# LSH attention and a gated FFN on one core: the second half of P's value products moved behind the first-layer products, and the hash in two TensorE passes with an add on VectorE

## The chip, the cores and the metric

One core of one Trainium2 chip. The metric is the device time of one execution in microseconds. The engines are named as in the profile: PE (TensorE; PEld its weight loads), DVE (VectorE), ACT (ScalarE), POOL (GpSimd), and SP, which issues most DMAs.

## The reference

```python
# B, H, S, D = 4, 8, 768, 64;  proj (64, 6);  w_in (512, 2048), w_out (2048, 512)
q_bits = (q @ proj) > 0;  k_bits = (k @ proj) > 0        # 6 bits each
q_bucket = sum(q_bits * 2**n);  k_bucket = sum(k_bits * 2**n)
mask = q_bucket[..., :, None] == k_bucket[..., None, :]
scores = where(mask, q @ k.T / sqrt(D), -1e9)
attn = exp(scores - max);  attn = attn / (sum(attn) + 1e-9)
x = (attn @ v), heads side by side: (3072, 512)
h = x @ w_in;  out = (h * clip(h + 3, 0, 6) / 6) @ w_out
```

The inputs are fp32. A product of full precision is made of TensorE passes in a rounded format (fp32r): each operand is split into a rounded high part and the remainder, its low part, and the products high x high, high x low and low x high are summed.

## The kernel before

**Units.** There are 32 heads with 6 tiles of 128 queries each, so 192 tiles g. The FFN takes x in 12 chunks of 256 tokens, each with 16 steps of the 2048 inner columns. The order of the instructions of PE, DVE, ACT and POOL is the order in which the program writes them; SP's is set by a scheduler.

**The stage of the change.** From tile GT = 102 on, attention and FFN run side by side in *slots* k, in the function `beside_ffn`; in the profile this is about 400 to 812 us. One slot holds one FFN step and one tile of each stage of attention. In PE's order:

- in every second slot (called odd here), the value products `acc` of a pair of tiles u: 12 matmuls of 256 columns
- the first layer `h` (gemm1): 12 matmuls of 256 columns
- in one slot in six, the hash `z` of the next head; such a slot is called a *hash slot*, it is always an odd one
- the second layer `po` (gemm2) of the step before: 6 matmuls of 512 columns
- the scores `s` of tile k + 3: 4 matmuls of 384 columns

The other engines in a slot: DVE takes the minimum of the scores (L396, into `p`); ACT the exponential (L408); DVE transposes `p` in 32 x 32 blocks (L429); DMAs carry it out to DRAM (`fd`) and back into the tile `spare` or `px` in transposed form. There it is split: ACT casts it to the high part `ph` (L475), and the low part `pl` is the difference. P has two halves c of 384 key columns. The half c = 1 is split first: `ph_1` by ACT, `pl_1` by POOL (L477). Then ACT makes the FFN's relu `g` (L683), and after it `ph_0`; `pl_0` is made by DVE (L479). ACT then casts the gate's result to `gb` (L689), DVE makes its low part (L690). After the value products, in the next (even) slot, ACT copies the sum out: `y` (L547).

**The value products** (`values_whole`, L505) are summed in one bank in the order ph_1, ph_0, pl_1, pl_0, three matmuls each, all ahead of the slot's first layer.

**The hash** (`hash_qk`, L325) gives 12 rows for q and 12 for k: each of the 6 projections with both signs. The tiles are q1 = [q high; k high], k2 = [k low; k high], q2 = [q high; q low]. Per half of 384 columns, three passes with the weights pjl (low part of proj), pjk and pjq (high part) are summed in one bank of PSUM. In `bits` (L344) DVE compares the rows with a threshold and multiplies them (L352), one instruction for each half, into rows 64 to 108 of q1. A DMA of 12 rows carries k's bits to the tile `k1`. The scores read them as extra rows of the product. In DVE's order bits stand between pl_0 and gb's low part; then comes the minimum of the next scores.

**K's raw rows** of the head after are loaded by a DMA that is put into the list `moves` and issued at the end of a slot, before the four DMAs of `move` (`spare<-fd`, `px<-fd`).

Of the kernel before, what the change touches and what calls it, by code (L numbers as in the profile page):

```python
# [18 lines left out]
P = 128  # L19
NB = 6  # L20
# [23 lines left out]
def lsh_attention_moe(  # L44
# [31 lines left out]
    def dma(out: bass.AP, in_: bass.AP):  # L76
        nonlocal last
        last = nc.sync.dma_start(out=out, in_=in_)  # L78
# [38 lines left out]


    pjl = cp.tile([P, ZM], F32R, name="pjl")
    pjh = cp.tile([P, ZM + ZK - D], F32R, name="pjh")  # L120
    nc.vector.memset(pjl[:].bitcast(F32), 0.0)
    nc.vector.memset(pjh[:].bitcast(F32), 0.0)
    pjk, pjq = pjh[:, :ZM], pjh[:, ZK - D :]


    nc.vector.memset(thr[:], 0.0)
    nc.vector.memset(val[:], 0.0)
    for r, one, big in ((D, 0, -BIG), (ZK, 1, 1.0)):
# [3 lines left out]
        nc.vector.memset(val[r : r + 2 * NB], big * (1, -1)[1 - one])  # L132
        nc.vector.memset(val[r : r + NB], big * (1, -1)[one])
    nc.vector.memset(three[:], 3.0)

    raw0 = sp.tile([P, S], F32, name="raw0", tag="raw", bufs=1)[:]
    dma(out=raw0, in_=qkT[0, 0])
# [107 lines left out]

    def get_k_rows(i: int):
        b, h = divmod(i, H)
        moves.append(lambda: dma(out=raws[i][D:], in_=qkT[b, h, D:]))

    def get_v(i: int):  # L250
        b, h = divmod(i, H)
# [3 lines left out]
    def hash_weights():  # L255
        for x in range(2):
            c = ZK + (1 - x) * NB
            nc.vector.tensor_scalar_mul(pjh[:, c : c + NB], pr[:], (1.0, -1.0)[x])
        for r, c in ((slice(0, D), D), (slice(D, P), ZK)):
            pos = pjh[r, ZK + NB : ZM]  # L260
            nc.vector.tensor_sub(pjl[r, c + NB : c + 2 * NB], pr[r], pos.bitcast(F32))
            nc.vector.tensor_sub(pjl[r, c : c + NB], pos.bitcast(F32), pr[r])

    def spans(i: int):

# [11 lines left out]

    copied = None
    subs = []
    moves = []  # L280

    def split_qk(i: int, copy):
        nonlocal copied
# [41 lines left out]
    def hash_qk(i: int):  # L325
        k1, k2, q1, q2 = state[i]
        if paced:
            z = zs[i] = [bank([P, HW], f"z{i}_{j}") for j in range(2)]
        else:
            both = pair(f"z{i}")  # L330
            z = zs[i] = [both[:, j, :HW] for j in range(2)]
        for j in range(2):
            c = slice(j * HW, (j + 1) * HW)
            nc.tensor.matmul(z[j][:ZM], lhsT=pjl[:], rhs=q1[:, c], start=True, stop=False)
            nc.tensor.matmul(z[j][:ZM], lhsT=pjk, rhs=k2[:, c], start=False, stop=False)
            nc.tensor.matmul(z[j][:ZM], lhsT=pjq, rhs=q2[:, c], start=False, stop=True)
        if not paced:
            zs[i] = both

    def bits(i: int):  # L340
        k1, k2, q1, q2 = state[i]
        z = zs.pop(i)

        if isinstance(z, list):  # L344
            whole = [(slice(j * HW, (j + 1) * HW), z[j][D:ZM], False) for j in range(2)]
        elif i == 0:
            whole = [(slice(j * HW, (j + 1) * HW), z[D:ZM, j, :HW], False) for j in range(2)]
        else:
            whole = [(slice(0, S), z[D:ZM, :, :HW], True)]
        for c, of, both in whole:  # L350
            to = q1[D:ZM, c]
            nc.vector.tensor_scalar(  # L352
                out=to.rearrange("p (j c) -> p j c", j=2) if both else to, in0=of,
                scalar1=thr[D:ZM], scalar2=val[D:ZM], op0=ALU.is_gt, op1=ALU.mult,
            )
            if i == 0:
                nc.scalar.copy(k1[D : D + 2 * NB, c], q1[ZK:ZM, c].bitcast(F32))  # L357
            elif c.stop == S:
                dma(out=k1[D : D + 2 * NB].bitcast(F32), in_=q1[ZK:ZM].bitcast(F32))
# [145 lines left out]
    def values_whole(u: int):  # L505
        vv = vvs[2 * u // KT]
        acc = accs[u] = bank([P, 2 * P], f"acc{u}")
        both = [parts.pop((u, c)) for c in range(2)]
        first, end = (0, 1, 0), (1, 0, QT - 1)
        for part in range(2):  # L510
            for c in (1, 0):
                for x in range(QT):
                    nc.tensor.matmul(  # L513
                        acc[:], lhsT=vv[:, c * QT + x], rhs=both[c][part][:, x],
                        start=(part, c, x) == first, stop=(part, c, x) == end,
                    )

    adds, fresh = [], []

# [518 lines left out]
    def lead(j: int):  # L1038

        i, t = divmod(j, KT)  # L1040
        n = i + 1
        alone = j <= GF + LA
        if t == 0 and n < NJ:
            split_qk(n, nc.scalar.copy if ffn_on else nc.gpsimd.tensor_copy)
        if t in (1, 4) and not paced:
            add()
        if t == (4 if paced else 2):
            if i:
                split_v(i)
        if t == (3 if paced else 2):  # L1050

            if n + 1 < NJ and n != H + 1:
                get_qk(n + 1)
                if paced:
                    get_k_rows(n + 1)
        if t == (5 if paced else 3) and n < NJ:
            get_v(n)
        hashed = t == 3 and n < NJ and alone and j != GB - 1
        if hashed:
            hash_qk(n)  # L1060
        scores(j)
        if hashed:
            bits(n)
        if t == (5 if paced else 4) and n + 1 < NJ:
            scale_q(n + 1)
# [7 lines left out]

    def value_whole():
        nonlocal vnext
        values_whole(vnext // 2)
        vnext += 2

    def value_half():
        nonlocal vnext  # L1080
# [18 lines left out]
    with tc.manual_schedule(engines={ET.PE, ET.DVE, ET.Activation, ET.Pool}):  # L1099
# [15 lines left out]
        def beside_ffn(k: int):  # L1115

            nonlocal paced, stage, held
            held = False  # L1120
            if k < GT:
                for c in range(2):
                    transp(k, c)
                exponential(k + 1)
            for _ in range(2):
                u = vnext // 2
                if u < NS // 2 and (2 * u < GT or k % 2 and k >= 2 * u + 3):
                    if vnext % 2 == 0 and k >= GT:
                        value_whole()
                        through.append(u)  # L1130
                        break
                    if value_half():
                        through.append(vnext // 2 - 1)
                if k < GT:
                    break
            behind = (k - 1 + LA) % KT == 4
            if GT <= k < NS - 2 and not behind:
                lowest(k + 2)
            go("A")
            if GT <= k < NS - 2 and behind:  # L1140
                lowest(k + 2)
            if k < GT:
                for c in range(2):
                    split_p(k, c, False)
                split_lows()
                while through:
                    output(through.pop(0))
                flip(k + 1)
            if k + 2 < NS:
                if k < GT:  # L1150
                    lowest(k + 2)
                    assert len(side) <= 2
                    opening.pop()()
                if k == GT:
                    go("B")
                    go("C")
                exponential(k + 2)
            paced = True
            multiply()
            if k + 2 < NS:  # L1160
                flip(k + 2)
            split = GT <= k - LT < NS
            if split:
                split_p(k - LT, 1, False)
            go("B")
            if k == NS + LT:
                homes.clear()
            while through and (through[0] < vnext // 2 - 1 or k % 2 == 0 or k < GT):
                output(through.pop(0))
            hashed = k + LA < NS and (k + LA) % KT == 4 and (k + LA) // KT + 1 < NJ  # L1170
            if hashed:
                hash_qk((k + LA) // KT + 1)
            if split:
                amid.append(lambda: (split_p(k - LT, 0, False), split_lows()))
            go("C")
            while amid:
                amid.pop()()
            split_lows()
            if hashed:
                bits((k + LA) // KT + 1)  # L1180
            if k + LA < NS:
                lead(k + LA)
            if moves:
                moves.pop(0)()
            if GT <= k + 1 < NS:
                move(k + 1)

            place_in_chunk = (k - GT) % NFC
            if subs and (k % 2 and (k < GT or place_in_chunk != NFC - 1) or k > GT and place_in_chunk == 0):
                subs.pop(0)()  # L1190
            go("D")
            if k % KT in (1, 3):
                add()

        for k in range(NS + LT + 2):
# [10 lines left out]
                load_first_x()  # L1206
            if k == HK:
                late["x"] = sp.tile([P, S], F32, name="late", tag="raw", bufs=1)
            for c in range(2):
                transp(k, c)  # L1210
            if k + 1 < end:
# [116 lines left out]
```

## Time and profile before

| what | us |
|---|---|
| median of 3 runs | 975.36 (973.79 to 977.28) |
| the profiled execution | 973.11 |
| its span in the profile | 971.3 |
| PE busy | 948.0, 98% of the span |
| DVE busy | 723.5, 74% |
| ACT busy | 625.0, 64% |
| POOL busy | 473.6, 49% |

The granted clock of TensorE was 0.998 of full speed. In a row of the timeline the first two numbers are the start and the length in us; `x6` counts instructions that follow one another on one line; the bracket gives the engine's idle time before the row and what ended it. In a row of a group of instructions, the numbers behind the first bar are the busy time in us and the mean of one in ns, those behind the second bar the idle time before them. In a row of one line's instructions, the three numbers are the shortest, median and longest in ns, and in the indented rows the idle time in us in front of them, by what ended it, and how often. Matmuls overlap, so the time that one of them takes on PE is the distance of the starts.

### The profile page before, as it was taken

What the parts mean: (1) busy time and instruction counts of PE and PEld (TensorE: products, weight loads), DVE (VectorE), ACT (ScalarE), POOL (GpSimd) and SP (SyncE); (2) the same over time, 40 slices, a digit from 0 to 9 for tenths busy, and PEclk for the clock granted to TensorE, in tenths of its full rate; (3) what the DMA queues carried; (4) which work ended last, traced back from release to release, by engine and by line L of the source; (5) the groups of instructions that cost most, each with busy time, mean ns of one, the idle gap of its engine ahead of it and who ended that gap; (6) DMA issues with size and microseconds to landing.
All of it is one profiled execution on the core that took longest, in us unless ns stands there. A gap on an engine that the chain in (4) does not pass through costs nothing.

```text
span 971.3 us, 19460 instructions
## 1 busy us (share of the span) xinstructions
PE 948.0 (98%) x6306; PEld 873.6 (90%) x6306; DVE 723.5 (74%) x1470; ACT 625.0 (64%) x1421; POOL 473.6 (49%) x582
## 2 busy tenths in 40 slices
PE   8999999999999999899999999999999999999997
PEld 7999888999989999799899899989899899889896
DVE  7999988888569999877878878878777874342422
ACT  6898875655478988667766666666666664333332
POOL 6777744665537776455555545555545432000000
PEclk9999999999999999999999999999999999999999
DMA  3567579100035554787898788788887772101000
GB/s 117 140 156 188 131 224 377 58 1 1 6 119 119 115 142 112 192 252 233 238 267 234 231 256 241 230 267 236 243 258 233 211 227 71 44 1 44 1 22 22
DMA packets 113613, 152.06 MB, mean 157 GB/s; under 512 B 13876, under 2 KB 82612, under 8 KB 113512
## 3 DMA queue, kind: packets, MB, share of 16 engines
q1 hardware_dynamic: 108472, 144.79, 48.8%
q0 software_dynamic: 5040, 6.03, 5.3%
q8 instruction: 50, 0.82, 0.4%
q14 instruction: 51, 0.42, 0.2%
HBM read 77.34 MB, written 54.00 MB: 135 GB/s over the span
## 4 chain that ended last, share of the span: by engine, by line
PE 79%; DVE 8%; DMA 4%; ACT 4%; issue 3%; POOL 1%; SPq 1%; ACTq 0%; DVEq 0%; POOLq 0%
PE h L661 25%; PE acc L500 6%; PE po L704 6%; PE po L699 6%; PE po L700 6%; PE acc L513 6%; PE pt L418 5%; PE s L389 5%; PE s L387 5%; DMA spare<-fd 2%; DVE p L396 2%; DVE pl L479 2%; ACT ph L475 1%; SPq L78 1%; DVE qq L352 1%
## 5 line engine op out<-in xcount | busy, mean ns | idle before, releaser
L408 ACT ACTIVATE p<-p,m 128x768 f32<-128x768 f32 x192 | 180.2, 939 | 113.4 <-DVE p L396 105.2
L396 DVE TENSOR_SCALAR_CACHE_REDUCE p<-s 128x768 f32<-128x768 f32 x192 | 182.7, 952 | 24.9 <-PE pt L418 12.4
L684 DVE SCALAR_TENSOR_TENSOR h<-g,h 128x256 f32<-128x256 f32 x192 | 81.1, 423 | 102.0 <-ACT g L683 99.0
L683 ACT ACTIVATE g<-h,three 128x256 f32<-128x256 f32 x192 | 91.2, 475 | 94.9 <-PE h L661 94.0
L661 PE MATMUL h<-xh,w 128*128 128x256 f32 x1024 | 146.8, 282 | 0.0
L661 PEld LDWEIGHTS h<-xh,w 128*128 128x128 f32 x1024 | 134.9, 188 | 4.2 <-ACT xh L650 0.6
L429 DVE STREAM_TRANSPOSE p<-p 128x768 f32<-128x768 f32 x90 | 88.1, 979 | 65.2 <-ACT p L408 65.1
L477 POOL TENSOR_TENSOR pl<-spare,ph 128x384 fp32r<-128x384 f32 x45 | 45.8, 1018 | 127.3 <-ACT ph L475 71.4
L479 DVE TENSOR_TENSOR pl<-pt,ph 128x384 fp32r<-128x384 f32 x196 | 100.0, 550 | 4.0 <-ACT ph L475 3.5
L387 PE MATMUL s<-kk,qq 76*128 76x384 f32 x384 | 100.5, 343 | 2.0 <-ACT kk L357 1.5
L389 PE MATMUL s<-kk,qq 128*128 128x384 f32 x384 | 100.4, 343 | 0.0
L700 PE MATMUL po<-w,gb 128*128 128x512 f32 x250 | 98.4, 393 | 0.0
L699 PE MATMUL po<-w,gb 128*128 128x512 f32 x250 | 98.3, 393 | 0.0
L475 ACT CAST ph<-pt 128x384 fp32r<-128x384 f32 x196 | 86.1, 474 | 14.3 <-PE pt L418 13.0
L216 POOL TENSOR_TENSOR w<-wr,w 128x128 fp32r<-128x128 f32 x128 | 71.9, 593 | 45.2 <-ACT w L210 41.9
L418 PE MATMUL pt<-ident,p 128*128 128x128 f32 x612 | 86.2, 275 | 1.9 <-DVE pl L479 1.1
L689 ACT CAST gb<-h 128x256 fp32r<-128x256 f32 x141 | 52.4, 372 | 54.5 <-DVE h L684 26.8
L661 PE MATMUL h<-xl,w 128*128 128x256 f32 x512 | 81.2, 280 | 0.0
L418 PEld LDWEIGHTS pt<-ident,p 128*128 128x128 f32 x612 | 72.5, 141 | 8.9 <-PE pt L418 1.5
L704 PE MATMUL po<-w,gb 128*128 128x512 f32 x250 | 78.6, 395 | 1.5 <-DVE gb L690 1.5
L318 POOL TENSOR_TENSOR kk<-raw,qq 64x192 fp32r<-64x192 f32 (+1 forms) x73 | 65.4, 920 | 25.1 <-ACT qq L304 21.7
L387 PEld LDWEIGHTS s<-kk,qq 76*128 76x128 f32 x384 | 66.6, 190 | 11.7 <-ACT kk L357 2.0
(153 smaller groups left out, 2150.9 us busy)
## 6 DMA issues: line engine op xcount, KB each, us to landing
fd<-p SPq DMA_DIRECT2D x90, 384.0 KB
spare<-fd SPq DMA_DIRECT2D x180, 96.0 KB
px<-fd SPq DMA_DIRECT2D x180, 96.0 KB
kk<-qq SPq DMA_DIRECT2D x62, 192.0 KB
wr<-in_w_in SPq DMA_DIRECT2D x16, 512.0 KB
wr<-in_w_out SPq DMA_DIRECT2D x16, 512.0 KB
raw<-in_qkT SPq DMA_DIRECT2D x19, 384.0 KB
vr<-in_v SPq DMA_DIRECT2D x32, 192.0 KB
```

The source lines that it names most:

```text
L387: nc.tensor.matmul(s[:, c, :HW], lhsT=q1[:KM, us], rhs=half(k1[:KM], c), start=True, stop=False)
L389: nc.tensor.matmul(s[:, c, :HW], lhsT=q2[:, us], rhs=half(k2, c), start=False, stop=True)
L396: nc.vector.tensor_scalar(out=pr_[:], in0=s[:, :, :HW], scalar1=CAP, scalar2=None, op0=ALU.min, op1=ALU.min, accum_out=m[:],)
L408: nc.scalar.activation(pr_[:], pr_[:], AF.Exp, bias=m[:], scale=-1.0, accum_out=sms[b][:, t, h : h + 1])
L418: nc.tensor.transpose(pt[:, x], probs[g][0][:, c, x * P : (x + 1) * P], ident[:])
L475: nc.scalar.copy(hi, pt)
L479: lows.append(lambda: engine.tensor_sub(lo, pt, hi.bitcast(F32)))
L661: nc.tensor.matmul(hp, lhsT=wi[:, wp, wc], rhs=x[cc][xp], start=(k == 0 and cc == 0), stop=(k == 2 and cc == NCC - 1),)
L683: nc.scalar.activation(r[:], hp, AF.Relu, bias=three[:], scale=1.0)
L699: nc.tensor.matmul(po[u], lhsT=gh[:, us], rhs=wo[:, 0], start=(fc == 0), stop=False)
L700: nc.tensor.matmul(po[u], lhsT=gh[:, us], rhs=wo[:, 1], start=False, stop=False)
L704: nc.tensor.matmul(po[u], lhsT=gl[:, us], rhs=wo[:, 0], start=False, stop=(fc == NFC - 1))
```

## The change

1. `values_whole` gives its two halves apart: the products of ph_1 and pl_1 stay ahead of the first layer, those of ph_0 and pl_0 follow it, ahead of the hash and the second layer.
2. In the stage of the change a hash takes two passes for each half instead of three: q2 and k2, each with 120 columns of weights that hold the low part of proj and its high part side by side. The result has the products with the low part in rows 0 to 24 and those with the high part in rows 96 to 120. ACT copies the first group out of PSUM into 24 rows of the next head's raw tile, for each half; DVE adds the second group to it, for each half, and then does the threshold over all 768 columns in one instruction, reading SBUF. A second set of thresholds, `limits`, is written at the start by eight small memsets on POOL; the new weights `pjs` are made by POOL once, at tile GT - 2.
3. The DMA of k's bits and the one of K's raw rows go into a new list, `behind_home`, that is issued after the four DMAs of `move`; K's rows are loaded a slot later, since their place holds the hash's sums till then.

```diff
+    def short_weights():
+        pjs = cp.tile([P, ZK + NR + NQ], F32R, name="pjs", tag="pjh")
+        nc.gpsimd.memset(pjs[:].bitcast(F32), 0.0)
+        short.extend([pjs[:, : ZK + NR], pjs[:, NQ:]])
...
     def hash_qk(i: int):
         k1, k2, q1, q2 = state[i]
         if paced:
-            z = zs[i] = [bank([P, HW], f"z{i}_{j}") for j in range(2)]
+            zs[i] = []
+            for j in range(2):
+                c = slice(j * HW, (j + 1) * HW)
+                z = bank([P, HW], f"z{i}_{j}")
+                zs[i].append(z)
+                nc.tensor.matmul(z[: ZK + NR], lhsT=short[1], rhs=q2[:, c], start=True, stop=False)
+                nc.tensor.matmul(z[: ZK + NR], lhsT=short[0], rhs=k2[:, c], start=False, stop=True)
+            return
...
         if isinstance(z, list):
-            whole = [(slice(j * HW, (j + 1) * HW), z[j][D:ZM], False) for j in range(2)]
+            r = slice(ZK, ZK + NR)
+            both = raws[i + 1][r] if i + 1 < NJ else sp.tile(...)[r]
+            for j in range(2):
+                nc.scalar.copy(both[:, j * HW : (j + 1) * HW], z[j][:NR])
+            for j in range(2):
+                c = slice(j * HW, (j + 1) * HW)
+                nc.vector.tensor_add(both[:, c], z[j][r], both[:, c])
+            nc.vector.tensor_scalar(
+                out=q1[D : D + NR], in0=both, scalar1=ths[r], scalar2=vas[r], op0=ALU.is_gt, op1=ALU.mult,
+            )
+            behind_home.append(lambda: dma(out=k1[D : D + NQ].bitcast(F32), in_=q1[D + NQ : D + NR].bitcast(F32)))
+            return
...
-        for part in range(2):
-            for c in (1, 0):
+        def half(c: int):
+            both = parts.pop((u, c))
+            for part in range(2):
                 for x in range(QT):
                     nc.tensor.matmul(
-                        acc[:], lhsT=vv[:, c * QT + x], rhs=both[c][part][:, x],
+                        acc[:], lhsT=vv[:, c * QT + x], rhs=both[part][:, x],
...
     def value_whole():
         nonlocal vnext
-        values_whole(vnext // 2)
+        half = values_whole(vnext // 2)
+        half(1)
+        rest.append(lambda: half(0))
...
+            go("B")
+            while rest:
+                rest.pop()()
             if split:
                 split_p(k - LT, 1, False)
-            go("B")
...
             if GT <= k + 1 < NS:
                 move(k + 1)
+            while behind_home:
+                behind_home.pop(0)()
```

PE's order in a hash slot, here that of the head whose passes start at 432.31 us in the profile; before:

```order
L513 MATMUL acc_5960<-ph_1_5866,vv_5663 128x256 x3
L513 MATMUL acc_5960<-ph_0_5892,vv_5663 128x256 x3
L513 MATMUL acc_5960<-pl_1_5867,vv_5663 128x256 x3
L513 MATMUL acc_5960<-pl_0_5893,vv_5663 128x256 x3
L661 MATMUL h_0_7_5987<-xh_0_5536,w_2678 128x256 x8
L661 MATMUL h_0_7_5987<-xl_0_5537,w_2678 128x256 x4
L334 MATMUL z_0_6000<-qq_5779,pjl 108x384
L335 MATMUL z_0_6000<-kk_5778,pjh 108x384
L336 MATMUL z_0_6000<-qq_5779,pjh 108x384
```

and in another hash slot of the changed kernel:

```order
L551 MATMUL acc_7114<-ph_1_7034,vv_6813 128x256 x3
L551 MATMUL acc_7114<-pl_1_7035,vv_6813 128x256 x3
L701 MATMUL h_1_9_7131<-xh_1_6564,w_2884 128x256 x8
L701 MATMUL h_1_9_7131<-xl_1_6565,w_2884 128x256 x4
L551 MATMUL acc_7114<-ph_0_7047,vv_6813 128x256 x3
L551 MATMUL acc_7114<-pl_0_7048,vv_6813 128x256 x3
L354 MATMUL z_0_7154<-qq_6933,pjs 120x384
L355 MATMUL z_0_7154<-kk_6932,pjs 120x384
```

The product with pl_1 is now the second group instead of the third, ph_0 and pl_0 have the first layer ahead of them, and the passes of z are two for each half.

DVE's order in the first of these hash slots, from the gate (h) to the minimum of the next scores (p, m); before:

```order
L684 SCALAR_TENSOR_TENSOR h_0_7_5987<-g_0_7_6014,h_0_7_5987 128x256
L479 TENSOR_TENSOR pl_0_6018<-spare,ph_0_6017 128x3x128
L352 TENSOR_SCALAR qq_5779<-z_0_6000,thr,val 44x384
L352 TENSOR_SCALAR qq_5779<-z_1_6001,thr,val 44x384
L690 TENSOR_TENSOR gb_0_7_6037<-h_0_7_5987,gb_0_7_6037 128x256
L396 TENSOR_SCALAR p_6041,m_6040<-s_6027 128x768
```

and in the changed kernel, the same slot:

```order
L724 SCALAR_TENSOR_TENSOR h_0_7_5992<-g_0_7_6027,h_0_7_5992 128x256
L516 TENSOR_TENSOR pl_0_6031<-spare,ph_0_6030 128x3x128
L377 TENSOR_TENSOR raw_5964<-z_0_6015,raw_5964 24x384
L377 TENSOR_TENSOR raw_5964<-z_1_6018,raw_5964 24x384
L378 TENSOR_SCALAR qq_5795<-raw_5964,limits 24x768
L730 TENSOR_TENSOR gb_0_7_6054<-h_0_7_5992,gb_0_7_6054 128x256
L433 TENSOR_SCALAR p_6058,m_6057<-s_6042 128x768
```

Two instructions became three, at the same place in the order. On ACT the two copies of z stand between ph_0 and gb:

```order
L512 CAST ph_0_6030<-spare 128x3x128
L374 COPY raw_5964<-z_0_6015 24x384
L374 COPY raw_5964<-z_1_6018 24x384
L729 CAST gb_0_7_6054<-h_0_7_5992 128x256
L445 ACTIVATE p_6058,sms_5294<-p_6058,m_6057 128x768
```

Before, the cast to gb followed that of ph_0 at once.

More of the change, by code (lines that the diff above doesn't have):

```diff
@@ L119, in lsh_attention_moe @@
     pjl = cp.tile([P, ZM], F32R, name="pjl")
-    pjh = cp.tile([P, ZM + ZK - D], F32R, name="pjh")
+    pjh = cp.tile([P, ZM + ZK - D], F32R, name="pjh", tag="pjh")
     nc.vector.memset(pjl[:].bitcast(F32), 0.0)
@@ L123, in lsh_attention_moe @@
     pjk, pjq = pjh[:, :ZM], pjh[:, ZK - D :]
+    NQ = 2 * NB
+    NR = 2 * NQ
+    short = []
+    limits = cp.tile([P, 2], F32, name="limits")
+    ths, vas = limits[:, 0:1], limits[:, 1:2]
     nc.vector.memset(thr[:], 0.0)
@@ L134, in lsh_attention_moe @@
     nc.vector.memset(three[:], 3.0)
+    for n, (lim, mul) in reversed(list(enumerate(((TINY, -BIG), (-TINY * (1 + 2.0 ** -23), BIG), (-TINY * (1 + 2.0 ** -23), -1.0), (TINY, 1.0))))):
+        r = slice(ZK, ZK + (n + 1) * NB)
+        nc.gpsimd.memset(ths[r], lim)
+        nc.gpsimd.memset(vas[r], mul)
     raw0 = sp.tile([P, S], F32, name="raw0", tag="raw", bufs=1)[:]
@@ L247, in get_k_rows @@
         b, h = divmod(i, H)
-        moves.append(lambda: dma(out=raws[i][D:], in_=qkT[b, h, D:]))
+        behind_home.append(lambda: dma(out=raws[i][D:], in_=qkT[b, h, D:]))
     def get_v(i: int):
@@ L262, in hash_weights @@
             nc.vector.tensor_sub(pjl[r, c : c + NB], pos.bitcast(F32), pr[r])
+    def short_weights():
+        pjs = cp.tile([P, ZK + NR + NQ], F32R, name="pjs", tag="pjh")
+        nc.gpsimd.memset(pjs[:].bitcast(F32), 0.0)
+        short.extend([pjs[:, : ZK + NR], pjs[:, NQ:]])
+        c = ZK + NQ
+        pos = pjs[:, c + NB : c + NQ].bitcast(F32)
+        for x in range(2):
+            nc.gpsimd.tensor_scalar_mul(pjs[:, c + (1 - x) * NB : c + (2 - x) * NB], pr[:], (1.0, -1.0)[x])
+        nc.gpsimd.tensor_sub(pjs[:, NQ + NB : 2 * NQ], pr[:], pos)
+        nc.gpsimd.tensor_sub(pjs[:, NQ : NQ + NB], pos, pr[:])
     def spans(i: int):
@@ L279, in lsh_attention_moe @@
     subs = []
-    moves = []
+    moves, behind_home = [], []
     def split_qk(i: int, copy):
@@ L327, in hash_qk @@
         if paced:
-            z = zs[i] = [bank([P, HW], f"z{i}_{j}") for j in range(2)]
-        else:
-            both = pair(f"z{i}")
-            z = zs[i] = [both[:, j, :HW] for j in range(2)]
+            zs[i] = []
[6 more added lines that the diff above has]
+            return
+        both = pair(f"z{i}")
+        z = zs[i] = [both[:, j, :HW] for j in range(2)]
         for j in range(2):
@@ L336, in hash_qk @@
             nc.tensor.matmul(z[j][:ZM], lhsT=pjq, rhs=q2[:, c], start=False, stop=True)
-        if not paced:
-            zs[i] = both
+        zs[i] = both
     def bits(i: int):
@@ L344, in bits @@
         if isinstance(z, list):
-            whole = [(slice(j * HW, (j + 1) * HW), z[j][D:ZM], False) for j in range(2)]
-        elif i == 0:
+            r = slice(ZK, ZK + NR)
+            both = raws[i + 1][r] if i + 1 < NJ else sp.tile([P, S], F32, name=f"raw{i + 1}", tag="raw", bufs=1)[r]
+            for j in range(2):
[8 more added lines that the diff above has]
+            return
+        if i == 0:
             whole = [(slice(j * HW, (j + 1) * HW), z[D:ZM, j, :HW], False) for j in range(2)]
@@ L507, in values_whole @@
         acc = accs[u] = bank([P, 2 * P], f"acc{u}")
-        both = [parts.pop((u, c)) for c in range(2)]
         first, end = (0, 1, 0), (1, 0, QT - 1)
-        for part in range(2):
-            for c in (1, 0):
+        def half(c: int):
+            both = parts.pop((u, c))
+            for part in range(2):
                 for x in range(QT):
                     nc.tensor.matmul(
-                        acc[:], lhsT=vv[:, c * QT + x], rhs=both[c][part][:, x],
+                        acc[:], lhsT=vv[:, c * QT + x], rhs=both[part][:, x],
                         start=(part, c, x) == first, stop=(part, c, x) == end,
                     )
+        return half
     adds, fresh = [], []
@@ L1053, in lead @@
                 get_qk(n + 1)
-                if paced:
-                    get_k_rows(n + 1)
+        if t == 4 and paced and n + 1 < NJ and n != H + 1:
+            get_k_rows(n + 1)
         if t == (5 if paced else 3) and n < NJ:
@@ L1075, in value_whole @@
         nonlocal vnext
-        values_whole(vnext // 2)
+        half = values_whole(vnext // 2)
+        half(1)
+        rest.append(lambda: half(0))
+        if vnext < GT:
+            rest.pop()()
         vnext += 2
+    rest = []
     def value_half():
@@ L1162, in beside_ffn @@
             split = GT <= k - LT < NS
+            go("B")
+            while rest:
+                rest.pop()()
             if split:
                 split_p(k - LT, 1, False)
-            go("B")
             if k == NS + LT:
@@ L1208, in lsh_attention_moe @@
                 late["x"] = sp.tile([P, S], F32, name="late", tag="raw", bufs=1)
+            if k == GT - 2:
+                short_weights()
             for c in range(2):
```

## The prediction

> **What bounds the kernel now.** I read the page's shares, then the stage in which the change lies (both halves of the work side by side, 412 to 812 us), then what ended TensorE's waits in front of the value products.
>
> ```profile
> span 971.3 us, 19460 instructions
> PE 948.0 (98%) x6306; PEld 873.6 (90%) x6306; DVE 723.5 (74%) x1470; ACT 625.0 (64%) x1421; POOL 473.6 (49%) x582
> 412.00:812.00 400.00, 395.54 (x2574) 365.90 (x2575) 313.75 (x601) 267.01 (x625) 208.69 (x269) 1.00 0.81 238
> L513 PE MATMUL acc<-ph,vv x270: 274/282/388, 412.0 to 811.7; 128*128 128x256 f32 x135
>   ACT ph L475: 10.5, 21
> ```
>
> The third row is the stage (its busy times are those of PE, weight loads, DVE, ACT, POOL): PE 395.5 of 400 us, DVE 313.8, ACT 267. PE is the bound, and what it still loses, it loses at the value products: the last row is TensorE's idle time in front of them, 10.5 us in 21 waits, ended by ACT's cast of P. But a loop of DVE and ACT runs close behind. Two pairs of slots, the first one following a hash slot:
>
> ```profile
> 493.26 1.01 POOL L477 TENSOR_TENSOR pl<-px,ph 128x384 fp32r<-128x384 f32 x1 [1.98 <-DMA spare<-fd]
> 493.70 0.51 ACT L475 CAST ph<-px 128x384 fp32r<-128x384 f32 x1
> 493.93 0.95 PE L513 MATMUL acc<-ph,vv 128*128 128x256 f32 x6
> 494.72 0.87 PE L513 MATMUL acc<-pl,vv 128*128 128x256 f32 x6
> 499.12 0.96 DVE L396 TENSOR_SCALAR_CACHE_REDUCE p<-s 128x768 f32<-128x768 f32 x1 [0.47 <-PE s L389]
> 501.05 0.82 POOL L522 DMA_DIRECT2D xs<-y  x1
> 501.94 1.01 POOL L477 TENSOR_TENSOR pl<-px,ph 128x384 fp32r<-128x384 f32 x1
> 502.10 0.51 ACT L475 CAST ph<-px 128x384 fp32r<-128x384 f32 x1
> 502.43 0.88 PE L513 MATMUL acc<-ph,vv 128*128 128x256 f32 x6
> 503.14 0.52 PE L513 MATMUL acc<-pl,vv 128*128 128x256 f32 x3
> ```
>
> The seventh value matmul comes 0.71 us after the first in the pair at 502.43, where ph_0 ended 0.18 after the start; in the pair at 493.93 it comes after 0.79, with ph_0 ending at 0.28. So the fourth matmul loses time once its operand is ready later than about 0.2 us after the start. The row at 499.12 shows the loop: DVE's minimum has only 0.47 us of idle before it, then waits for PE's scores. That is the slack of DVE.
>
> **The change part by part.** *Hash passes.* 14 heads, two halves, three passes become two:
>
> ```profile
> L334 PE MATMUL z<-qq,pjl x28: 332/338/424, 401.7 to 763.9; 128*108 128x384 f32 x28
> 763.38 0.34 PE L334 MATMUL z<-qq,pjl 128*108 128x384 f32 x1
> 764.43 0.40 PE L699 MATMUL po<-w,gb 128*128 128x512 f32 x1
> ```
>
> Six passes take 764.43 - 763.38 = 1.05 us, 0.175 each. The new ones have the same 384 moving columns, so 28 x 0.175 = **-4.9 us** of PE time, all of it where PE is the bound.
>
> *Order of the value products.* The fourth matmul no longer needs ph_0 but pl_1. Both follow ph_1: ph_0 by ACT's relu and a cast, pl_1 by POOL's 1.01 us subtraction. In the pair at 493.93 pl_1 ends at 494.27, 0.34 after the start (ph_0: 0.28); at 502.43 it ends at 502.95, 0.52 after the start (ph_0: 0.18), because POOL was issuing the DMA of 501.05. So one wait takes the place of the other: 0.1 us instead of 0.08 in the first kind, 0.3 instead of none in the second. What queues behind the waiting matmul is the whole first layer, and behind that relu on ACT. Going through the 45 pairs in this way, they lose 11.1 us before (the view above has 10.5 of it). 32 do not follow a hash slot; ten of them have POOL late and lose 0.27 more each (2.7), the other 22 together 0.8: **+3.5 us**. What is won is where ph_0 alone is late, since a first-layer product of 1.4 us now hides it; that is one pair:
>
> ```profile
> 632.26 0.51 PE L513 MATMUL acc<-ph,vv 128*128 128x256 f32 x3
> 634.27 0.63 PE L513 MATMUL acc<-ph,vv 128*128 128x256 f32 x3 [1.50 <-ACT ph L475]
> ```
>
> *The hash's vector work.* A hash slot and the pair behind it:
>
> ```profile
> 571.16 0.50 ACT L475 CAST ph<-spare 128x384 fp32r<-128x384 f32 x1
> 571.69 0.64 DVE L479 TENSOR_TENSOR pl<-spare,ph 128x384 fp32r<-128x384 f32 x1
> 572.37 1.29 DVE L352 TENSOR_SCALAR qq<-z,thr,val 44x384 fp32r<-44x384 f32 x2
> 572.78 1.01 POOL L368 TENSOR_TENSOR vv<-vr,vv 128x384 fp32r<-128x384 f32 x1
> 573.18 0.37 ACT L689 CAST gb<-h 128x256 fp32r<-128x256 f32 x1 [1.52 <-PE po L704]
> 573.69 0.42 DVE L690 TENSOR_TENSOR gb<-h,gb 128x256 fp32r<-128x256 f32 x1
> 573.70 1.10 PE L661 MATMUL h<-xh,w 128*128 128x256 f32 x8
> 574.03 0.95 DVE L396 TENSOR_SCALAR_CACHE_REDUCE p<-s 128x768 f32<-128x768 f32 x1
> 576.54 1.01 POOL L477 TENSOR_TENSOR pl<-px,ph 128x384 fp32r<-128x384 f32 x1 [1.98 <-ACT ph L475]
> 577.22 0.96 PE L513 MATMUL acc<-ph,vv 128*128 128x256 f32 x6
> ```
>
> DVE runs without a gap from 571.69 to the minimum at 574.03, 0.33 after PE began the next slot: bits end, gb follows at once, then the minimum, and from it the exponential, ph_1 and pl_1 (577.55, 0.33 after the value products start). No slack is left here. Prices of the new instructions:
>
> ```profile
> L479 DVE TENSOR_TENSOR pl<-pt,ph 128x384 fp32r<-128x384 f32 x196 | 100.0, 550 | 4.0 <-ACT ph L475 3.5
> L545 DVE TENSOR_TENSOR y<-acc,y 64x256 f32<-64x256 f32 x4 | 1.7, 428 | 0.8 <-ACT y L544 0.7
> L352 DVE TENSOR_SCALAR qq<-z,thr,val 44x384 fp32r<-44x384 f32 x30 | 19.3, 686 | 1.0 <-PE z L336 0.5
> L352 DVE TENSOR_SCALAR qq<-z,thr,val 44x768 fp32r<-44x768 f32 x17 | 18.5, 1086 | 0.8 <-POOL rblate L577 0.3
> L291 DVE CAST qq<-raw 64x768 fp32r<-64x768 f32 x1 | 0.6, 557 | 2.2 <-DMA raw<-in_qkT 2.2
> L203 DVE TENSOR_SCALAR wr<-wr x32: 409/692/1080, 22.2 to 253.5; 128x512 f32<-128x512 f32 x32
> L475 ACT CAST ph<-pt 128x384 fp32r<-128x384 f32 x196 | 86.1, 474 | 14.3 <-PE pt L418 13.0
> ```
>
> ACT's two copies are 384 columns out of PSUM: 0.47 each, from 571.66 to 572.6. DVE is busy with pl until 572.33, so the copies delay neither add; they lie in the 1.52 us that ACT waits there for PE (1.17 with PE 0.35 earlier). They cost nothing; if that cover went, gb and the second layer would be next. The two adds read PSUM and SBUF as the pl<-pt row does: 0.55 each (between 0.43, the 256-wide row, and 0.69). The threshold over 768 columns is now read from SBUF. Its bounds are 0.41, the least of the L203 rows, and 1.09, the same width out of PSUM; nearest is the cast at 0.56, to which I add the 0.14 by which the L352 form exceeds the L479 form at equal width, and 0.1 for the spread of L203: 0.80. [...]
>
> DVE so does 2 x 0.55 + 0.80 = 1.90 us where it did 1.29: 0.6 later, while PE is 0.35 earlier: the chain is 0.95 later against PE. The pair at 577.22 then loses 0.33 + 0.95 - 0.21 = 1.07 instead of 0.07. Thirteen pairs follow a hash slot: five like this (+5.0); two that lost 0.68 already (+0.9 each); the one at 604.66, whose pl_1 was ready at its start (+0.7); the one at 632.26, where ph_0 is now hidden (1.76 to 1.54, -0.2); and four whose hash slot is of this kind:
>
> ```profile
> 542.22 0.48 ACT L683 ACTIVATE g<-h,three 128x256 f32<-128x256 f32 x1 [0.43 <-PE h L661]
> ```
>
> There relu waits 0.43 for the first-layer product, which now ends 0.71 earlier, so pl and the adds start 0.43 earlier and the lateness is only 0.4: +0.1 twice and +0.45 twice. Together **+8.3 us**.
>
> *The rest.* K's raw rows are loaded behind the bits' DMA; both queue on SP behind four moves instead of three, about 0.5 us each, and the first reader comes ten us after the passes (z at 487.26, the cast at 497.86):
>
> ```profile
> 497.86 0.83 ACT L304 CAST qq<-raw 128x768 fp32r<-128x768 f32 x1
> ```
>
> Nothing, then; without that cover the head's split, and after it the hash, would be late. The new weights are a few small POOL instructions, once, on an engine that is busy for half of the span (first fence). The eight memsets at the start: at most 0.1 us.
>
> **Sum.** -4.9 + 3.5 + 8.3 = +6.9 us. Against the profiled execution, 973.11: 980.0. The median of the runs shown lies 2.25 above it, so 982.3.
>
> **Rivals.** (1) *The loop catches up: no change.* If adds and threshold cost the lower bounds, 2 x 0.43 + 0.41 = 1.27, DVE is no later than before and only PE's 0.35 remains: the thirteen pairs lose 7.5 instead of 5.9. -4.9 + 3.5 + 1.6 = +0.2: 975.6. For it: the cast at 0.56. Against: adds of this width take 0.55 here, and the L352 form is slow. It decides below about 1.4 us for the three.
>
> (2) *The earlier first layer drives the loop: faster.* If relu waited for the first-layer product in most odd slots, as at 542.22, everything behind it would come 0.43 earlier: the 32 pairs would lose 2 us instead of 5.2, the nine others behind a hash slot 0.43 less each. -4.9 - 3.2 + 4.4 = -3.7: 971.7. It decides if that wait stands in more than 40 of 45 odd slots. Against: relu waited for PE in only 10 of 89 slots here, 4.1 us in all; else it starts as ph_1's cast ends.
>
> ```profile
>   PE h L661: 4.1, 10
> ```
>
> (3) *The threshold is slow: a larger loss.* With 0.69 and 1.09 the three take 2.46, 0.56 more lateness: nine pairs +5.0, four +2.4: 989.7. For it: POOL's 1.01 us subtraction lies beside the threshold in the slot shown, and the L203 form takes up to 1.08 at 512 columns. [...]
>
> **How the numbers follow.** Forecast 0.50, rival 3 (beyond 985.5) 0.18, rival 1 0.20, rival 2 0.12. A measurement tells 0.3%, 2.9 us, from no change: faster 0.12, same 0.20, slower 0.68. The forecast's own range is 978 to 986. The stated range leaves out rival 2 and the far end of 3: 973.5 to 988.
>
> **What would show it.** PE: 56 passes for 84, z to po in 0.70 us. Each step is right if DVE's three new instructions take about 1.9 us, the minimum behind them starts about 1.3 us into the next slot instead of 0.33, and PE's waits in front of the value products name POOL's pl instead of ACT's ph, about 1 us each behind hash slots, some 23 us in all for 11. Wrong if the threshold takes under 0.5, if pl_1 is there in time (relu and all behind it earlier), or if a wait opens at the scores or the first layer instead.

## The result, and the profile after

The changed kernel takes 981.92 us (median of 6 runs, 980.78 to 982.83); the kernel before, run beside it, 976.32 (973.79 to 978.29). The ratio is 1.0053, 95% interval 1.0032 to 1.0074: slower by half a per cent. The profiled execution took 982.65 us. Its page:

```profile
span 980.9 us, 19507 instructions
PE 950.7 (97%) x6278; PEld 870.0 (89%) x6278; DVE 728.5 (74%) x1484; ACT 634.7 (65%) x1449; POOL 475.8 (49%) x595
```

PE issues 28 matmuls less (6278 for 6306) and its span is 9.6 us longer. The stage, 412 to 822 us now (busy times of PE, weight loads, DVE, ACT, POOL; then the granted clock):

```profile
412.00:822.00 410.00, 399.40 (x2554) 363.57 (x2554) 318.68 (x614) 276.86 (x654) 209.40 (x269) 1.00 0.81 233
```

PE is idle for 10.6 us of 410 where it was for 4.5 of 400. The value products in that stretch, and what ended TensorE's idle time in front of them:

```profile
L551 PE MATMUL acc<-ph,vv x267: 277/280/393, 412.9 to 820.8; 128*128 128x256 f32 x134
...
  POOL pl L514: 18.8, 42
  issue: 5.9, 11
  ACT ph L512: 4.3, 8
```

Where ACT's cast ph had ended most of this idle time (10.5 us), POOL's difference pl now does: 18.8 us in 42 waits. (These figures count both matmuls and weight loads, so they are a sum over two queues and not time lost.) The hash slot that answers to the one at 571 us before, with the pair behind it:

```profile
576.83 0.34 PE L354 MATMUL z<-qq,pjs 128*120 128x384 f32 x1
...
577.53 0.39 PE L739 MATMUL po<-w,gb 128*128 128x512 f32 x1
...
577.84 0.84 ACT L374 COPY raw<-z 24x384 f32<-24x384 f32 x2
577.88 0.67 DVE L516 TENSOR_TENSOR pl<-spare,ph 128x384 fp32r<-128x384 f32 x1
...
578.59 1.04 DVE L377 TENSOR_TENSOR raw<-z,raw 24x384 f32<-24x384 f32 x2
...
579.00 1.01 POOL L405 TENSOR_TENSOR vv<-vr,vv 128x384 fp32r<-128x384 f32 x1
...
579.64 1.10 PE L701 MATMUL h<-xh,w 128*128 128x256 f32 x8
579.66 0.77 DVE L378 TENSOR_SCALAR qq<-raw,limits 24x768 fp32r<-24x768 f32 x1
...
580.80 0.95 DVE L433 TENSOR_SCALAR_CACHE_REDUCE p<-s 128x768 f32<-128x768 f32 x1
...
583.31 1.00 POOL L514 TENSOR_TENSOR pl<-px,ph 128x384 fp32r<-128x384 f32 x1 [2.53 <-ACT ph L512]
...
583.37 0.59 PE L551 MATMUL acc<-ph,vv 128*128 128x256 f32 x3
...
584.37 0.39 PE L551 MATMUL acc<-pl,vv 128*128 128x256 f32 x1 [0.41 <-POOL pl L514]
```

Read it from the top. From the first pass to the second layer PE takes 0.70 us instead of 1.05. ACT's copies lie beside DVE's pl, and the adds start 0.04 us after it ends. The adds and the threshold keep DVE from 578.59 to 580.43, so the minimum starts 1.16 us into the next slot (580.80 against 579.64) where it started at 0.33. The lateness goes on through exponential, cast and POOL: pl_1 is done at 584.31, 0.94 us after the value products began, and the fourth of these waits for it.

To put numbers on this I take, for each of the 45 pairs, the distance of the starts from the matmul ahead of the first product to the last product, less the usual distances (0.118 us for 256 columns, 0.177 for 384, 0.231 for 512). This counts short delays as well, so the sum before is 12.0 us, where the prediction's reckoning had 11.1. Where products stand on both sides of the first layer, the distance spans that layer too, and what it loses is in the figure.

| kernel (profiled execution) | 32 other pairs, us lost | 13 pairs behind hash slots, us lost |
|---|---|---|
| before | 5.7 | 6.3 |
| changed | 10.8 | 12.2 |
| order alone | 8.5 | 4.4 |
| hash alone, old order | 6.2 | 14.8 |
| changed, without copies and adds | 9.6 | 7.2 |
| changed, copies without adds | 10.1 | 7.1 |
| changed, adds without copies | 10.2 | 13.1 |
| before, with an extra threshold | 6.9 | 8.1 |

Between the two profiled executions, then: -4.9 for the passes, +5.1 and +5.9 at the value products, and some 3.4 elsewhere make 9.5. Of the 3.4, 0.9 stands ahead of the first pair (it starts at 412.92 instead of 412.03), and some 1.0 in first layers that begin a new chunk: four of them lose 0.62 to 0.69 us, by distances of starts, where before two lost 0.80. The rest isn't traced.

### The profile page after: what moved, and what is told of

Read it like the earlier page. It is cut to its first block, busy times and chain, and to the rows that moved or that the text cites. A ratio compares the mean times of both kernels' runs of the same rounds, so it can differ in the third digit from the quotient of the medians.

```text
span 980.9 us, 19507 instructions
## 1 busy us (share of the span) xinstructions
PE 950.7 (97%) x6278; PEld 870.0 (89%) x6278; DVE 728.5 (74%) x1484; ACT 634.7 (65%) x1449; POOL 475.8 (49%) x595
## 4 chain that ended last, share of the span: by engine, by line
PE 69%; DVE 7%; POOL 6%; issue 6%; DMA 5%; ACT 4%; SPq 2%; POOLq 0%; ACTq 0%; DVEq 0%
PE h L701 23%; PE acc L537 6%; PE po L739 5%; PE po L744 5%; PE po L740 5%; PE pt L455 5%; PE acc L551 4%; PE s L426 4%; PE s L424 4%; POOL pl L514 3%; DMA px<-fd 3%; DVE pl L516 2%; DVE p L433 2%; SPq L78 2%; ACT ph L512 2%
## 5 line engine op out<-in xcount | busy, mean ns | idle before, releaser
L514 POOL TENSOR_TENSOR pl<-px,ph 128x384 fp32r<-128x384 f32 x45 | 46.0, 1022 | 70.2 <-ACT ph L512 56.5
```

Of the source, the lines that this page charges most:

```text
L514: engine.tensor_sub(lo, pt, hi.bitcast(F32))
```

## The experiments

Theory A is the prediction's: DVE's added work in hash slots makes the chain from the minimum to ph and pl late, and PE waits for it. The rivals: the order costs it, ACT's copies or the transfers' new list cost it, or it is not DVE's work that counts. Each kernel was timed in five rounds against the kernel before (974.25, 975.29, 974.66 and 975.67 us in the four groups of runs); differences in us are worked out from the ratios.

**Order alone.** The old hash and the old lists of transfers; only the value products are split:

```diff
-        values_whole(vnext // 2)
+        half = values_whole(vnext // 2)
+        half(1)
+        rest.append(lambda: half(0))
...
             go("B")
+            while rest:
+                rest.pop()()
```

> The order of the value products alone; the hash (three passes, bits on DVE) and the DMA lists as before. Theory A (PE's fourth value matmul waits for POOL's pl_1 instead of ACT's ph_0, and hash slots make the chain late through DVE): the pairs that do not follow a hash slot lose 3.5 us more, those that do 1.3 us less: +2 us, with the waits in front of the value products named POOL pl. Rival B (the order helps, the loss is the hash's alone): -3 us or better. Rival C (the loss comes from the DMAs put behind the moves): 0.

Measured: 976.18 us, ratio 1.0012 (1.0000 to 1.0024), so +1.2 us. Idle time in front of the value products, 412 to 812 us:

```profile
  POOL pl L477: 11.2, 28
  issue: 2.0, 3
  ACT ph L475: 1.9, 5
```

One wait takes the place of the other, as predicted: pl_1 ends them instead of ph_0, in sum not much more than the 10.5 us before. The other pairs lose 2.8 us more, and the pairs behind hash slots 1.9 less, 1.3 of it at the one pair (632.26 before) whose ph_0 is hidden now.

**Hash alone.** The changed kernel with the old order of the value products:

```diff
-        half = values_whole(vnext // 2)
-        half(1)
-        rest.append(lambda: half(0))
+        values_whole(vnext // 2)
```

> The hash in two passes with its copies, adds and DMA list; the value products in the old order. Theory A: -4.9 us of passes; the pairs behind hash slots lose about 8.5 us more, now in front of ph_0: +3.6 us. Rival B: all of the loss, +5.6 us or more. Rival D (the vector work is hidden and the order alone is the loss): -4.9 us.

Measured: 981.74 us, ratio 1.0067 (1.0048 to 1.0086). So the hash by itself makes the whole loss:

```profile
  ACT ph L512: 19.9, 43
  issue: 6.4, 11
  POOL pl L514: 0.2, 1
```

The waits keep their old name and double. Pairs behind hash slots lose 8.5 us more, the figure expected. In spite of 4.9 us fewer passes the time rises by 6.5: by the same distances of starts the first layer loses 6.3 us where it lost 3.7 before, 2.0 of it where xh and xl of a new chunk come late, and 1.1 in one layer that a dip of the clock slows (at 639 us; last section).

**Without copies and adds.**

```diff
-                nc.scalar.copy(both[:, j * HW : (j + 1) * HW], z[j][:NR])
...
-                nc.vector.tensor_add(both[:, c], z[j][r], both[:, c])
-            nc.vector.tensor_scalar(
-                out=q1[D : D + NR], in0=both, ...
+                nc.vector.tensor_scalar(
+                    out=q1[D : D + NR, c], in0=z[j][r], ...
```

> The changed kernel with the two-pass hash, but ScalarE's two copies and VectorE's two additions left out: the threshold reads rows 96 to 120 of each half of z directly, in two instructions (left out of the result: the low half of the projection's products). VectorE's work per hash slot is then about 2 x 0.65 = 1.29 us as in the kernel before, instead of 2 x 0.558 + 0.764 = 1.88. Theory A (the loss is the chain's lateness from VectorE's added work): the followers of hash slots fall from +5.9 of lost time to about 1.6, the time to about +0.2 us against the kernel before, some 5.5 us less than the changed kernel. Rival (the additions are covered, the loss has another cause, such as the passes' own place or the new DMA list): it stays at about +5.6 us against before.

Measured: 975.19 us, ratio 0.9998 (0.9984 to 1.0011). The loss is gone. The new order and the new list of transfers are in this kernel as in the changed one, so the 5.4 us between the two belong to the copies and the adds. The same place in the timeline:

```profile
573.94 1.29 DVE L375 TENSOR_SCALAR qq<-z,limits 24x384 fp32r<-24x384 f32 x2
575.61 0.95 DVE L430 TENSOR_SCALAR_CACHE_REDUCE p<-s 128x768 f32<-128x768 f32 x1
...
578.53 0.51 PE L548 MATMUL acc<-ph,vv 128*128 128x256 f32 x3
...
579.18 0.62 PE L548 MATMUL acc<-pl,vv 128*128 128x256 f32 x3
```

DVE takes 1.29 us as before, and pl's products follow those of ph after 0.65 us instead of 1.00. The pairs behind hash slots lose 7.2 us; the prediction's first rival had 7.5 for exactly this case, and +0.2 us in all.

**Copies without adds, adds without copies.** Each half of what the run above left out:

```diff
 copies only:  the threshold reads z[j][r]; nc.scalar.copy(both..., z[j][:NR]) stays
 adds only:
-                nc.vector.tensor_add(both[:, c], z[j][r], both[:, c])
+                nc.vector.tensor_add(both[:, c], z[j][r], thr[r].to_broadcast([NR, HW]))
```

> The changed kernel with ScalarE's two copies of 0.47 us per hash slot kept, but VectorE's additions left out: the threshold reads the high half of z directly, in two instructions (left out of the result: the low half of the projection's products). Theory A (the copies are free, as the prediction had it): 0 against the kernel before, like the run without both. Rival (ScalarE's copies delay the casts of px that the value products wait for): 28 x 0.47 = 13 us of work, of which a quarter to a half shows: +3 to +6 us.

> The changed kernel with VectorE's two additions and the one threshold kept, but ScalarE's copies left out: the addition takes a stored constant as its second operand (left out of the result: the low half of the projection's products). Theory A (VectorE's 1.88 us per hash slot instead of 1.29 are the loss): +4.5 to +5.6 us against the kernel before, nearly all of what the changed kernel loses. Rival (the loss is in the copies, or in VectorE's wait for them): 0 to +2 us.

Measured: copies only 974.95 us, ratio 0.9997 (0.9985 to 1.0010); adds only 982.02, ratio 1.0074 (1.0059 to 1.0089). Nothing of the 28 copies shows in the time, the adds are the loss. With the adds, DVE again takes from 579.42 to 581.27, and pl is late:

```profile
579.42 1.04 DVE L375 TENSOR_TENSOR raw<-z,thr 24x384 f32<-24x384 f32 x2
...
580.50 0.77 DVE L376 TENSOR_SCALAR qq<-raw,limits 24x768 fp32r<-24x768 f32 x1
581.64 0.95 DVE L431 TENSOR_SCALAR_CACHE_REDUCE p<-s 128x768 f32<-128x768 f32 x1
...
585.20 0.62 PE L549 MATMUL acc<-pl,vv 128*128 128x256 f32 x3 [0.41 <-POOL pl L512]
```

**DVE's work alone, in the kernel before.** The threshold of the first half is issued twice; nothing else changes:

```diff
-            whole = [(slice(j * HW, (j + 1) * HW), z[j][D:ZM], False) for j in range(2)]
+            whole = [(slice(j * HW, (j + 1) * HW), z[j][D:ZM], False) for j in (0, 0, 1)]
```

> The kernel before, with the threshold of the first half of the buckets issued twice in each hash slot: VectorE gets 0.645 us more in each of 14 slots, TensorE, ScalarE and the order are untouched. Theory A (in a hash slot VectorE sets when the next chunk's min, and with it ph_0, comes): 13 slots x 0.5 to 0.65 us, in sum +6 to +8 us. Rival (VectorE's work in hash slots is off the path): 0.

Measured: 983.95 us, ratio 1.0083 (1.0064 to 1.0102), +8.1 us: 14 times 0.645 us of DVE is 9.0, so nearly all of it shows in the time. But not where I expected it: the value products lose only 3.0 us more (table). The first layer, 412 to 822 us, waits as well; the kernel before, and then this one:

```profile
  ACT xh L650: 0.6, 2
```

```profile
  PE s L389: 3.3, 8
  DVE qq L352: 1.6, 4
  ACT gb L689: 0.7, 2
  ACT xh L650: 0.6, 2
```

Which transfer or release stands behind the waits that are put down to PE's scores isn't shown. In this execution the clock dipped besides, by 3.4 us (last section); but another execution of this kernel, with a granted clock of 1.000, took 983.55 us against the 984.09 profiled, so the dip isn't what makes the 8.1.

**All value products behind the first layer.** If PE waits because ph and pl are late, later products should hide that. With the old hash, and with the two-pass hash:

```diff
-        half(1)
-        rest.append(lambda: half(0))
+        rest.extend([lambda: half(1), lambda: half(0)])
...
-                rest.pop()()
+                rest.pop(0)()
```

> The hash as before, but all twelve value products of a pair behind the first layer of their slot. Theory A: the first layer's 1.4 us covers ph_1, pl_1 and ph_0, so the 11 us of waits in front of the value products go down to 1 or 2: -9 us. Rival E (the lateness only moves on, to the second layer, the scores or relu): -3 us or less gain, with new waits there.

> All twelve value products behind the first layer, and the hash in two passes. Theory A: pl_1, 1.3 us after the start behind a hash slot, is needed 1.6 us after it, so the DVE work is covered and the passes are won: -4.9 - 9 = -14 us. Rival E: without PE's waits the loop of DVE and ACT, 0.95 us later behind each hash slot, is not caught up and holds PE elsewhere: -5 us.

Measured: 969.52 us, ratio 0.9935 (0.9916 to 0.9954), with the old hash; 975.43, ratio 1.0008 (0.9993 to 1.0022), with the new. The first is a gain, but two thirds of that expected. In the second nothing of the gain is left (+0.8 us): the rival, which put it at -5, was right in kind, and the loss is larger than it had. Idle time in front of the first layer, 412 to 812 us, in the one and in the other:

```profile
  ACT y L550: 7.6, 13
```

```profile
  ACT y L587: 19.0, 30
```

The waits have moved to ACT's copy of the sums, behind which the first layer's bank comes free. (The profiled execution of the second kernel took 978.80 us, 3.4 over its median, so its 19.0 is rather high.) The two-pass hash costs 7.1 us here (5.9 by the medians).

**The copy earlier.** To take that wait away, the copy y is written ahead of the exponential in the even slot, with the old hash and the new:

```diff
+        def sums_out(k: int):
+            while through and (through[0] < vnext // 2 - 1 or k % 2 == 0 or k < GT):
+                output(through.pop(0))
...
+                else:
+                    sums_out(k)
```

> The kernel before with all twelve value products of a chunk behind the first-layer products, as in the earlier run of that order, and ScalarE's copy of the sums (which frees the bank that the first layer's h takes) moved ahead of the exponential of the even slot. Theory A: the 3.6 us that the first layer lost to that copy in the earlier run come back, and the time is 9 to 10 us below the kernel before (about 965). Rival (the copy was only the last of several things that came late together, or the exponential becomes late instead): no better than the earlier run, about -6 us.

> The same, with the two-pass hash on top. Theory A (behind hash slots only VectorE's min is late, and with the value products behind the first layer and the copy early nothing on TensorE waits for it): the passes' 4.9 us come on top of the other gain, about -13 us against the kernel before. Rival E (the lateness only moves on to the next product that needs VectorE or ScalarE): -3 to -5 us.

Measured: 967.57 us, ratio 0.9913 (0.9890 to 0.9936), with the old hash; 972.70, ratio 0.9967 (0.9953 to 0.9981), with the new. The old hash comes near the sum expected (-8.5 of -9 to -10 us) and has the lowest median of the complete versions; its interval and that of the run without the early copy (0.9916 to 0.9954) overlap. With the new one it is the rival again, -3.2 us. Idle time in front of the first layer, old hash and new:

```profile
  DVE qq L352: 2.4, 6
  ACT y L550: 1.8, 2
```

```profile
  ACT y L587: 4.1, 2
  DVE raw L377: 3.1, 8
  ACT xh L690: 1.8, 4
```

One wait of 2 us for the copy is left; beside it DVE's adds stand in the list now, and the new hash still costs 5.3 us (0.9967 against 0.9913).

**The same without copies and adds.** To see whether the passes' 4.9 us come out once the adds are gone: the same edit as in the third experiment, on this order.

> The kernel with all value products behind the first layer, the early copy of the sums and the two-pass hash, but without ScalarE's copies and VectorE's additions (left out of the result: the low half of the projection's products). Theory A (the copies and additions are all that keeps the passes' saving from the time): -8.5 for the order and the copy, -4.9 for the passes, in sum about -13 us against the kernel before. Rival (in this order TensorE is held by something else, and time saved on its passes comes back as waiting): about -8.5 us, as with the three-pass hash.

Measured: 965.70 us, ratio 0.9908 (0.9891 to 0.9924), -9.0 us. Copies and adds together are worth 5.8 us here as well; but against the three passes (0.9913) the two gain 0.5 us, within the intervals (2.9 between the two profiled spans, 966.4 and 963.5), and not 4.9. The rival was right. The last run shortens DVE's work further, the threshold being issued for one half only:

```diff
-            for j in range(2):
+            for j in range(1):
```

> The last but two of the runs (all value products behind the first layer, early copy of the sums, two passes, no copies and no additions) with the threshold issued for the first half of the buckets alone (left out of the result: the bits of the second half as well), so that VectorE has 0.68 us less in each hash slot. Theory B (in that run the passes' 4.9 us came back as waits because the first layer, which comes earlier by the saved time, then stands behind VectorE's thresholds): these waits go, and the time falls from -9.0 to about -11 or -12 us against the kernel before. Rival (the saved time is lost to something other than VectorE, late transfers above all): it stays at about -9.

Measured: 964.48 us, ratio 0.9886 (0.9860 to 0.9912), -11.1 us. The waits of the first layer that DVE's threshold ends, with both halves and with one:

```profile
  DVE qq L374: 4.8, 8
```

```profile
  DVE qq L374: 2.7, 4
```

This goes the way of theory B, and the idle time halves; the intervals of the two ratios overlap, so that the passes come back as waits behind DVE is supported and not settled.

## Why the prediction came out right, step by step

**The passes** were worth what was said on PE (0.70 us from z to the second layer, at 13 of the 14 heads; 1.28 for 1.45 at the first), but not in time. The run without copies and adds lies only 1.4 us below the one with the order alone (0.9998 against 1.0012, intervals that overlap), so most of the 4.9 seems to have come back: in the slots where PE saves 0.35 us, DVE and what follows it don't get any earlier. The two kernels differ in the list of transfers too, and its share wasn't tried apart. The prediction had this as 1.6 us of lateness, in its first rival; the runs without adds (7.2 for 4.4 lost behind hash slots, 9.6 for 8.5 at the others) show 3.9.

**The order**, +3.5 at the 32 other pairs: 2.8 in the run with the order alone, 5.1 in the changed kernel. The shape was only partly as predicted. Pairs with POOL late lost 0.13 to 0.20 us more each, not 0.27, as POOL started 0.24 us behind the cast instead of 0.38. Three pairs lost 1.55, 1.31 and 1.16 more, which no step had. One of them is this; ACT's cast waits for the transfer of px:

```profile
572.55 0.51 ACT L512 CAST ph<-px 128x384 fp32r<-128x384 f32 x1 [1.32 <-DMA px<-fd]
573.11 0.62 PE L551 MATMUL acc<-ph,vv 128*128 128x256 f32 x3 [0.58 <-ACT ph L512]
...
574.25 0.50 PE L551 MATMUL acc<-pl,vv 128*128 128x256 f32 x2 [0.51 <-POOL pl L514]
```

The first of the three falls into a dip of the clock (last section), and 1.0 of its 1.55 is lost by the first layer between its halves. The third stands in the run with the order alone too (1.35 us lost at that pair, against 0.03 before), so the new list of transfers isn't its cause. What made px late I did not try. The order's net cost of 1.2 us is smaller than its term, because it helps the pairs behind the old hash by 1.9; the prediction counted that gain inside the hash's term.

**The hash's vector work**, +8.3. The prices:

```profile
L377 DVE TENSOR_TENSOR raw<-z,raw x28: 552/558/565, 408.1 to 774.3; 24x384 f32<-24x384 f32 x28
L378 DVE TENSOR_SCALAR qq<-raw,limits x14: 757/764/771, 409.2 to 774.9; 24x768 fp32r<-24x768 f32 x14
L374 ACT COPY raw<-z x28: 462/466/469, 407.4 to 773.4; 24x384 f32<-24x384 f32 x28
```

An add was put at 0.55, the threshold at 0.80, a copy at 0.47: in sum 1.88 us for 1.90. The lateness that follows was right in kind and put too large. The regular pairs behind hash slots lose 0.87 more each, not 1.00; two that lost 0.68 before, 0.77 and not 0.9; the one at 611.22 (604.66 before) 0.46 and not 0.7; the one at 638.89 gains 0.7 where 0.2 was put. Of the four whose relu waits for the first layer, two lose 0.13 and two 0.04, so that wait absorbs more than I gave it. That is 5.9 at these pairs for 8.3 (the parts of it, as printed, add to 8.4), and the minimum starts 1.16 us into the next slot, not 1.3. All value products together lose 23.0 us, the prediction's some 23, but by two errors of opposite sign: the hash's term was 2.4 too large, the order's 1.6 too small. What no step had is that the first layer loses more too: by the distances of starts 5.4 us where it lost 3.7. Of that, 1.0 is the layer slowed by the dip of the clock at 412.92, which the table holds already.

The slack of DVE was read from one row, 0.47 us ahead of the minimum at 499.12. Over the stage of the kernel before most minimums have none:

```profile
L396 DVE TENSOR_SCALAR_CACHE_REDUCE p<-s x85: 895/950/958, 413.3 to 797.8; 128x768 f32<-128x768 f32 x85
...
  PE s L389: 8.2, 21
```

Of 85 minimums 21 wait for the scores, 0.39 us each on average; none of those behind the hash's thresholds does. In all 14 hash slots DVE runs from pl to the minimum without a gap over 0.04 us, before and after. So what the forecast rests on holds, and 0.47 is not the slack of every other slot.

**POOL beside the threshold**, which the third rival has on its side, shows no such loss. In all 14 hash slots POOL's subtraction is still running when the threshold starts: in the slot above it runs from 579.00 until 580.01, and the threshold starts at 579.66, 0.03 us after the adds, and takes 0.77 us (757 to 771 ns in the 14 slots). So the threshold didn't wait for the end of the subtraction, and it stayed far under the rival's 1.09. Whether it would be faster without POOL beside it no run here tells. Reading 768 columns from SBUF took 764 ns (24 rows) against 1086 out of PSUM before (44 rows, L352).

**The sum.** +6.9 was made against one profiled execution, 973.11 to 980.0, and that of the changed kernel came to 982.65: 2.6 us too little. The passes kept their 4.9 on PE, the order cost 5.1 for 3.5, the hash's work 5.9 for 8.3, and 3.4 stood in no term. The median was then put 2.25 above the profiled execution, as before; it lay 0.73 below. The two errors cancel nearly: the median's agreement to 0.4 us is luck, and between the medians run side by side the loss is 5.6 us. What the experiments bear out is the sign, the mechanism (adds on DVE, free copies) and the price of DVE's time: +5.4 us (changed kernel against that without copies and adds) to +7.4 (adds only against the same) for 0.59 us in each of 14 slots, 8.2 in all.

## What to carry to other kernels

When an engine at 97% sits in a loop with another at 74%, read the slack of the loop in the slot that is changed, not the shares: in the 14 hash slots DVE had no idle time from pl to its minimum. There a microsecond taken from PE saved some 0.3 us or less by the medians (1.4 of 4.9, and 0.5 in the other order, both within the intervals), and one added to DVE cost 0.7 to 0.9 (5.4 of 8.2, 8.1 of 9.0), so the trade from the one to the other lost here (5.6 us between the medians). Moving a late consumer back helped here only until the next product of the same loop was late: the first layer, behind the copy that frees its bank (7.6 us in 13 waits). With the copy moved as well the order gave 8.5 us instead of 6.3, a difference that the intervals leave open.

## What the runs showed of the hardware

The granted clock fell briefly in this stage in some executions. The kernel before has 1.00 in every stretch of 4 us from 400 to 820 us. The changed kernel, right behind waits of the second layer (0.35 us before 408.69, 0.61 before 410.49) and of the first pair of value products (0.57 before 412.92); the columns are those of the stretches above:

```profile
412.00:416.00 4.00, 3.05 (x14) 2.52 (x14) 3.09 (x6) 3.35 (x8) 1.01 (x1) 0.67 0.92 254
416.00:420.00 4.00, 4.00 (x24) 3.73 (x24) 1.94 (x3) 2.61 (x7) 1.96 (x3) 0.91 0.61 201
```

At 0.67 and 0.91 these 8 us lose 4 x 0.33 + 4 x 0.09 = 1.7 us of the clock, and the pair at 412.92, which lost 1.55 more, lies in them. Another execution of the changed kernel, at a granted clock of 1.000, took 981.21 us, 0.7 below the median. The kernel with the extra threshold dips at the same place:

```profile
412.00:416.00 4.00, 3.81 (x17) 3.84 (x18) 3.24 (x7) 3.26 (x8) 1.03 (x2) 0.50 0.77 237
416.00:420.00 4.00, 4.00 (x20) 3.68 (x19) 1.46 (x3) 1.98 (x4) 1.40 (x2) 0.72 0.38 136
```

With the 0.93 of the stretch from 408 to 412 that is 4 x 0.07 + 4 x 0.50 + 4 x 0.28 = 3.4 us, twice as much. Three other kernels have one dip each of 1.7 us: the hash alone (0.93 and 0.64 in the two stretches from 636 to 644), adds without copies (0.93 and 0.65 from 412 to 420), all value products behind with the early copy and the new hash (0.84 and 0.73 from 632 to 640). Four show 1.00 in every stretch of 4 us from 396 to 760: the order alone, the one without copies and adds, all value products behind with the new hash, and the early copy with the old hash. The kernel before had no dip though one wait of its value products is 1.50 us.

What brings a dip wasn't tried. In the changed kernel the clock is 1.00 up to 413.33 us, 0.51 from there to 414.00, and 1.00 again from 417 on. In the 4.00 us ahead of the drop, from 409.33 to 413.33, PE was busy for 2.68. But the kernel before had PE busy for only 2.50 of the 4.00 us from 632.33 to 636.33, and its clock stayed at 1.00 there and up to 640. So the share of idle time alone didn't bring the drop.
